# Odd batches tiled from token 64 in a sliding-window attention and spectral-mixing kernel

## The chip, the cores and the metric

The kernel runs on one core of one Trainium2 chip. The metric is the device time of one execution in microseconds. The engines are called as in the profile: PE (matmul), PEld (its weight loads, which overlap PE), DVE, ACT, POOL, and SP, which here only issues DMAs. A profile's times count from the start of its span.

## The reference

There are 8 batches, 8 heads, 576 tokens and a head width of 64. Each token attends to itself and the 127 before it, with a bias that falls off linearly with distance. The result x (8 x 576 x 512) is then mixed along the sequence in 64 Fourier modes:

```python
scores = scale * q @ k.T
mask = (rel >= 0) & (rel < 128)               # rel = query position - key position
scores = where(mask, scores - slope[h] * |rel|, -1e9)
x = softmax(scores) @ v                       # heads side by side: 8 x 576 x 512
X = rfft(x, axis=1)                           # of which 64 modes are kept
Y[:, m] = X[:, m] @ (w_r[m] + 1j * w_i[m])    # 64 complex matrices of 512 x 512
u = x + irfft(Y)
out = u + relu(u @ w_ch)
```

The weights w_r and w_i are 64 x 512 x 512 in float32 each, most of the 164 MB that are read.

## The kernel before

**Tiles of tokens.** 576 tokens are four tiles of 128 and one of 64. `g.x_sb` holds the four whole tiles of each batch, `g.x4` the rest: the last 64 tokens of an even batch in its partitions 0 to 63, those of the next, odd batch in 64 to 127. `g.seq` lists the 36 tiles in the order in which the tail works on them, with batch and first token of each half. `g.F` is the Fourier matrix with tokens on the partitions, one block of 128 for each tile; `g.FT` is its transpose for the way back, from which the tail takes 64 columns for each half of a tile.

**Attention.** A unit is two heads of one batch; there are 32, and batches go in pairs. For each pair d there are two slots (n = 2d and 2d + 1), in which `_slot` writes the work out by hand in this order on PE: scores of the first head (L436, after a filler matmul L417 that keeps PE going), transposes of the next pair's q and k (L377), transposes of v (L406), scores of the second head, more transposes, one batch's part of the spectrum (`_spectrum1`, L526), and `_av` (L467) for the pair before, the even batch in the even slot and the odd batch in the odd one. ACT does the exponential of the scores (L442) and copies most transposes out of PSUM (L387), DVE multiplies by the mask (L450) and divides by the sums (L483 to L489), POOL casts the loaded q, k and v to bf16 (L367). Scores have one PSUM buffer, and each engine works in the order written.

**`_av`.** A tile of 128 queries needs two tiles of keys: its own and the one before. So there are two matmuls for each tile and head but the first, each of 128 columns of attention (the stationary operand) and 65 columns of v with a column of ones. In the odd slot the shared tile follows: 64 columns for each batch, to partitions 0 to 63 and 64 to 127. That makes 14 matmuls in an even slot and 22 in an odd one.

**Weights.** They come through `g.wring`, a ring of three buffers of 18 KB per partition, filled by `_send` from SP's queue, in order with the loads of q, k and v (L356). Mode matrices for the first 128 channels are used during attention (`_modes`, L672, L620); the other three quarters follow in `_pair` (L703, L629) after it, while PE also transposes x (L726) and multiplies it with w_ch (L748).

**Tail.** After the last weights, `_finish` goes through the 36 tiles. Place i of the list decides how its result is added ("a": ACT and DVE; "q": ACT, DVE and POOL). `store` issues its stores on SP (L840, 256 KB; for a shared tile two of 128 KB, L842). The constants are set up once in `_consts` and `_consts2`.

Of the kernel before, what the change touches and what calls it, by code (L numbers as in the profile page):

```python
# [10 lines left out]
BF16 = mybir.dt.bfloat16  # L11
# [5 lines left out]
P = 128  # L17
# [16 lines left out]
def kernel(  # L34
# [10 lines left out]
    nc = tc.nc  # L45
    B, H, S, D = q.shape
    NM, DM, _ = moe_w_r.shape
# [3 lines left out]
    g = Ctx()  # L51
# [26 lines left out]

    g.FT = persist.tile([P, 4, S], BF16)
    g.F = persist.tile([P, ST, P], BF16)  # L80
    g.ident_b = persist.tile([P, P], BF16)
    g.ident2 = persist.tile([P, 64], BF16)
    g.wch = persist.tile([P, 4, DM], BF16)
# [5 lines left out]
    g.spectra = []  # L89
    g.seq = []  # L90
    for b in range(B):
        g.seq += [(g.x_sb[:, b, st], ((b, st * P), (b, st * P + 64))) for st in range(4)]
        if b % 2:
            g.seq.append((g.x4[:, b // 2], ((b - 1, 4 * P), (b, 4 * P))))
    g.way = ["q" if 2 <= i < len(g.seq) - 5 and i % 5 in (0, 2, 3) else "a" for i in range(len(g.seq))]

    with tc.manual_schedule(engines={ET.SP, ET.PE, ET.Activation, ET.DVE, ET.Pool}):
# [122 lines left out]
def _consts(g, tp):  # L220
    nc = g.nc
    NM, S, ST = g.NM, g.S, g.ST
    pi = tp.tile([P, 1], I32)
    nc.gpsimd.iota(pi, [[0, 1]], base=0, channel_multiplier=1)
    mi = tp.tile([P, 2, NM], I32)
    nc.gpsimd.iota(mi, [[0, 2], [1, NM]], base=0, channel_multiplier=0)
    make_identity(nc, g.ident_b)
    FAR = float(2**15)
    rel = tp.tile([P, 512], FP32)
    g.rel = rel  # L230
    both = rel.rearrange("p (a b) -> p a b", a=2)
    nc.gpsimd.iota(both, [[0, 2], [1, 256]], base=0, channel_multiplier=-1,
                   allow_small_or_imprecise_dtypes=True)
    for sign, base in ((1, 0), (-1, P - 1)):
        nc.gpsimd.affine_select(
            out=both, in_=both, compare_op=ALU.is_ge, fill=FAR, base=base,
            pattern=[[0, 2], [sign, 256]], channel_multiplier=-sign)
    tail = rel[:, 448:512]
    nc.gpsimd.iota(tail, [[1, 64]], base=64, channel_multiplier=-1,
                   allow_small_or_imprecise_dtypes=True)  # L240
    for base, step, mul in ((64, 1, -1), (-64, 0, 1)):
        nc.gpsimd.affine_select(
            out=tail, in_=tail, compare_op=ALU.is_ge, fill=FAR, base=base,
            pattern=[[step, 64]], channel_multiplier=mul)
    g.heads = list(range(1, g.H))

    pcol = tp.tile([P, 1], FP32)
    nc.vector.tensor_copy(pcol, pi)
    mrow = tp.tile([P, 2, NM], FP32)
    nc.vector.tensor_copy(mrow, mi)  # L250
    scol = tp.tile([P, ST], FP32)
    for st in range(ST):
        nc.vector.tensor_scalar_add(scol[:, st : st + 1], pcol, float(st * P))
    nc.vector.tensor_scalar_add(scol[64:128, 4:5], pcol[64:128], float(4 * P - 64))
    phrow = tp.tile([P, 2, NM], FP32)
    nc.vector.memset(phrow[:, 0, :], S / 4.0)
    nc.vector.memset(phrow[:, 1, :], S / 2.0)
    MAGIC = float(2**23)
    ang = tp.tile([P, ST * P], FP32)
    for st in range(ST):  # L260
        nc.vector.scalar_tensor_tensor(
            out=ang[:, st * P : (st + 1) * P],
            in0=mrow.rearrange("p a b -> p (a b)"),
            scalar=scol[:, st : st + 1], op0=ALU.mult,
            in1=phrow.rearrange("p a b -> p (a b)"), op1=ALU.add,
        )
    kf = tp.tile([P, ST * P], FP32)
    nc.vector.tensor_scalar_mul(kf, ang, 1.0 / S)
    nc.vector.tensor_scalar(kf, kf, MAGIC, -MAGIC, op0=ALU.add, op1=ALU.add)
    nc.vector.scalar_tensor_tensor(  # L270
        out=ang, in0=kf, scalar=-float(S), op0=ALU.mult, in1=ang, op1=ALU.add)
    nc.scalar.activation(
        g.F.rearrange("p a b -> p (a b)"), ang, AF.Sin, scale=2.0 * math.pi / S)
    g.one = pcol


def _consts2(g):
    nc = g.nc
    nc.gpsimd.tensor_tensor(
        out=g.ident2, in0=g.ident_b[:, 0:64], in1=g.ident_b[:, 64:128], op=ALU.add)  # L280
    nc.gpsimd.memset(g.pick, 0.0)
    one = g.ident_b.rearrange("p (q t) -> p q t", t=2)
    for h in range(2):
        for t in range(2):
            nc.gpsimd.tensor_copy(
                g.pick[:, h, t].rearrange("p (q t) -> p q t", t=2)[:, :, t], one[:, :, h])
    for vn in g.vns:
        nc.gpsimd.memset(vn[:, :, :, g.D : g.D + 1], 1.0)

# [163 lines left out]
def _av(g, d, e, av):  # L453


    nc = g.nc
    u = g.two[d]
    _, s, b = g.units[2 * d + e]
    D = g.D
    vn = g.vns[d % 2]  # L460

    def part(t, f, h, o, **kw):
        m = P if t < 4 else 64
        terms = [(t - 1, 256 * ((t - 1) % 2) + P)] if t else []
        terms.append((t, 256 * (t % 2) if t < 4 else 448))
        for i, (kt, c0) in enumerate(terms):
            nc.tensor.matmul(  # L467
                av[o, h, t * (D + 1) : (t + 1) * (D + 1)],
                lhsT=u.att[min(kt // 2, 1), h][:, f, c0 : c0 + m],
                rhs=vn[:, g.ST * h + kt, f, 0 : D + 1],  # L470
                start=(i == 0), stop=(i == len(terms) - 1), **kw)

    for h in range(2):
        for t in range(4):
            part(t, e, h, slice(0, P))
    n = 4 + e
    if e:
        for h in range(2):
            for f in range(2):
                part(4, f, h, slice(64 * f, 64 * f + 64), tile_position=(0, 64 * f))  # L480
    avv = av[:, :, 0 : n * (D + 1)].rearrange("p h (t c) -> p h t c", t=n)
    rec = g.work.tile([P, 2, n], FP32, tag=f"rec{e}", name="rec")
    nc.vector.reciprocal(rec, avv[:, :, :, D])  # L483
    xo = g.x_sb[:, b, :, s * P : (s + 1) * P].rearrange("p t (h d) -> p h t d", h=2)
    nc.vector.tensor_tensor(  # L485
        out=xo, in0=avv[:, :, 0:4, 0:D],
        in1=rec[:, :, 0:4].unsqueeze(-1).broadcast_to([P, 2, 4, D]), op=ALU.mult)
    if e:
        nc.vector.tensor_tensor(  # L489
            out=g.x4[:, b // 2, s * P : (s + 1) * P].rearrange("p (h d) -> p h d", h=2),  # L490
            in0=avv[:, :, 4, 0:D],
            in1=rec[:, :, 4].unsqueeze(-1).broadcast_to([P, 2, D]), op=ALU.mult)
# [10 lines left out]
def _spectrum1(g, j, b, a):  # L503

    nc = g.nc
    grp = GROUPS[j]
    ST = g.ST
    A = len(grp)
    po = 64 * (b % 2)
    ps = slice(po, po + 64)  # L510
    X = g.X[j]
    nb = 4 // A
    own = b == g.B - 1
    if own and a == 0:
        sc = g.ps2.tile([P, 2, 512], FP32, tag="sc", name="xtl")
        g.xt2 = sc[:, 0, 0 : A * 2 * g.NM].rearrange("p (k a i m) -> p k a i m", k=1, a=A, i=2)
    elif b % nb == 0 and a == 0:
        g.xt = g.ps2.tile([P, nb, A, 2, g.NM], FP32, tag="xt", name="xt")
    xt = g.xt2 if own else g.xt
    k = 0 if own else b % nb  # L520
    dc = slice(grp[0] * P + a, grp[0] * P + A * P, A)
    for st in range(ST):
        l = g.x_sb[:, b, st, dc] if st < 4 else g.x4[ps, b // 2, dc]
        f = g.F[:, st] if st < 4 else g.F[ps, st]
        kw = {} if st < 4 else dict(tile_position=(po, 0))
        nc.tensor.matmul(  # L526
            xt[:, k, a].rearrange("p i m -> p (i m)"), lhsT=l, rhs=f,
            start=(st == 0), stop=(st == ST - 1), **kw)
    if a < A - 1 or not own and b < g.B - 2 and k < nb - 1:
        return  # L530
    b0 = b - k
    if j:
        nc.vector.tensor_copy(X[:, :, :, b], xt[:, 0])
        return
    xi = xt[:, 0 : k + 1, 0].rearrange("p b i m -> p i b m")
    nc.vector.tensor_copy(X[:, 0, 1:3, b0 : b + 1], xi)
    nc.vector.tensor_scalar_mul(X[:, 0, 0, b0 : b + 1], xi[:, 1], -1.0)
# [283 lines left out]
def _finish(g):  # L821
# [5 lines left out]
    with ExitStack() as fctx:  # L827
        pool = fctx.enter_context(tc.tile_pool(name="fin", bufs=4))
        lps = fctx.enter_context(
            tc.tile_pool(name="lps", bufs=1, space=bass.MemoryType.PSUM, side="right"))  # L830
        first = [min(i for i, t in enumerate(g.seq) if t[1][0][0] == b and t[1][1][0] == b)
                 for b in range(g.B)]
        _z_late(g, 0, lps)
        _z_take(g, 0)
        o, r, y = {}, {}, {}

        def store(i):
            for h, (b, s) in enumerate(g.seq[i][1]):
                if h == 0 and g.seq[i][1][1] == (b, s + 64):
                    nc.sync.dma_start(out=g.out[b, s : s + P, :], in_=o[i])  # L840
                    break
                nc.sync.dma_start(out=g.out[b, s : s + 64, :], in_=o[i][64 * h : 64 * h + 64])  # L842

        for i in range(N + 3):
            if i < N:
# [62 lines left out]
```

## Time and profile before

| what | value |
|---|---|
| median of three runs | 444.44 us (443.52 to 445.49) |
| profiled execution | 445.46 us, its span 443.7 us |
| busy of the span | PE 72%, PEld 46%, DVE 50%, ACT 48%, POOL 23% |
| DMA | 173.73 MB, mean 392 GB/s |
| attention | to about 161 us (last L467) |
| weights of the other channels | to about 403 us |
| tail | from there to the end |
| matmuls on L467 | 576 |
| stores | 32 of 256 KB, 8 of 128 KB |

The shares of the span are means over three stages with different limits, so each stage has to be read by itself: in the windows view for its engines, and in the chain of waits for what ended last.

### The profile page before, as it was taken

To read this page: it belongs to the slowest core of one execution; us is meant where nothing else is said; L and a number is where in the kernel's file an instruction comes from. 1 tells how busy PE (TensorE), PEld (TensorE's weight loads), DVE (VectorE), ACT (ScalarE), POOL (GpSimd) and SP (SyncE) were. 2 spreads that over 40 slices of the span, in tenths; PEclk is the share of its full clock that TensorE was granted. 3 is DMA by queue.
4 is the path that set the end of the run, shared out by engine and by line. 5 is a ranking of instruction groups with operands and counts; after the bars stand their busy time and mean duration, and the time that the engine had idled before them with its cause. 6 is when DMAs were issued, how large, how long until landed. Compare 5 with 4: busy or idle time off the path is not lost.

```text
span 443.7 us, 10963 instructions
## 1 busy us (share of the span) xinstructions
PE 319.0 (72%) x4647; PEld 205.0 (46%) x4675; DVE 221.7 (50%) x404; ACT 214.8 (48%) x332; POOL 103.1 (23%) x156
## 2 busy tenths in 40 slices
PE   2778889899979878557564565554675587688994
PEld 1445566667757654334332333332333355344552
DVE  6466867778748723343332333323333345413784
ACT  4799968999969603222232212222122133302883
POOL 8844535555534102000000000000000000000882
PEclk9999978999969965687766858768658589966998
DMA  8999989999999999999999999999999999991787
GB/s 285 394 392 403 404 319 390 406 407 405 406 407 382 405 420 425 410 426 430 430 427 428 430 429 422 427 427 418 434 427 427 428 419 429 425 421 71 256 313 263
DMA packets 46145, 173.73 MB, mean 392 GB/s; under 512 B 3984, under 2 KB 3984, under 8 KB 38032
## 3 DMA queue, kind: packets, MB, share of 16 engines
q1 hardware_dynamic: 46096, 173.03, 96.9%
q8 instruction: 36, 0.59, 0.5%
q14 instruction: 13, 0.11, 0.1%
HBM read 163.58 MB, written 9.44 MB: 390 GB/s over the span
## 4 chain that ended last, share of the span: by engine, by line
DMA 56%; PE 21%; ACT 12%; DVE 6%; issue 3%; SPq 0%; POOL 0%; ACTq 0%; POOLq 0%
DMA wring<-in_moe_w_i_dram 33%; DMA wring<-in_moe_w_r_dram 23%; ACT att L442 5%; PE acc L703 4%; ACT T L387 4%; PE mm L735 3%; DVE att L450 2%; PE sc L436 2%; PE tqk L377 2%; PE y L735 2%; PE av L467 2%; PE acc L672 2%; PE av L406 1%; DVE x_sb L485 1%; ACT ys L865 1%
## 5 line engine op out<-in xcount | busy, mean ns | idle before, releaser
L752 ACT CAST hl<-xw 64x512 bf16<-64x512 f32 x72 | 41.7, 579 | 139.5 <-PE xw L748 101.2
L703 PE MATMUL acc<-Xz,wring 128*128 128x32 bf16 x1536 | 51.4, 183 | 72.1 <-DMA wring<-in_moe_w_i_dram 37.5
L703 PEld LDWEIGHTS <-wring 128*128 128x128 bf16 x1536 | 45.6, 101 | 103.9 <-DMA wring<-in_moe_w_i_dram 54.9
L753 DVE TENSOR_TENSOR hl<-xw,hl 64x512 bf16<-64x512 f32 x72 | 49.6, 688 | 79.2 <-ACT hl L752 79.0
L874 POOL TENSOR_TENSOR o<-r,ys 128x512 f32<-128x512 f32 x18 | 22.5, 1274 | 242.6 <-ACT ys L865 241.5
L450 DVE TENSOR_TENSOR att<-att,mask 128x1024 bf16<-128x1024 bf16 x64 | 55.2, 863 | 37.4 <-ACT att L442 36.8
L442 ACT ACTIVATE att<-sc 128x1024 bf16<-128x1024 f32 x64 | 67.0, 1047 | 10.0 <-PE sc L436 8.8
L387 ACT COPY T<-tqk 128x640 bf16<-128x640 bf16 x92 | 65.9, 773 | 1.7 <-PE tqk L377 1.7
L748 PE MATMUL xw<-wch,xT 128*128 128x512 bf16 x119 | 48.1, 522 | 4.7 <-issue 2.9
L377 PE MATMUL tqk<-ident_b,b 128*128 128x128 bf16 x432 | 39.5, 233 | 10.9 <-POOL b L367 6.4
L377 PEld LDWEIGHTS <-b 128*128 128x128 bf16 x432 | 27.3, 103 | 22.5 <-issue 11.0
L728 DVE COPY xT<-tp 128x512 bf16<-128x512 bf16 x36 | 15.1, 420 | 34.3 <-PE tp L726 34.2
L367 POOL CAST b<-v 128x576 bf16<-128x576 f32 x32 | 27.0, 869 | 16.4 <-issue 9.0
L436 PE MATMUL sc<-T,T 64*128 64x256 bf16 (+2 forms) x320 | 26.7, 264 | 2.3 <-ACT att L442 1.8
L367 POOL CAST b<-q 128x576 bf16<-128x576 f32 x32 | 21.4, 697 | 28.6 <-issue 28.6
L748 PEld LDWEIGHTS <-xT 128*128 128x128 bf16 x144 | 17.8, 129 | 21.3 <-issue 17.2
L367 POOL CAST b<-k 128x576 bf16<-128x576 f32 x32 | 22.0, 713 | 16.9 <-issue 8.7
L467 PE MATMUL av<-vn,att 128*128 128x65 bf16 (+1 forms) x576 | 24.5, 201 | 0.7 <-DVE x L489 0.4
L672 PE MATMUL acc<-X,wring 128*128 128x16 bf16 x488 | 18.9, 193 | 5.6 <-DMA wring<-in_moe_w_i_dram 5.2
L485 DVE TENSOR_TENSOR x_sb<-av,rec 128x512 bf16<-128x512 f32 x32 | 22.1, 691 | 1.1
L467 PEld LDWEIGHTS <-att 128*128 128x128 bf16 (+1 forms) x576 | 20.6, 104 | 3.7 <-DVE x L489 0.5
L406 PE MATMUL av<-ident_b,T 128*128 128x128 bf16 x160 | 15.1, 227 | 8.7 <-DVE x_sb L485 5.2
(106 smaller groups left out, 430.4 us busy)
## 6 DMA issues: line engine op xcount, KB each, us to landing
wring<-in_moe_w_r_dram SPq DMA_DIRECT2D x32, 1536.0 KB, 10.1
wring<-in_moe_w_i_dram SPq DMA_DIRECT2D x31, 1536.0 KB, 10.1
wring<-in_moe_w_i_dram SPq DMA_DIRECT2D x22, 768.0 KB, 8.9
wring<-in_moe_w_r_dram SPq DMA_DIRECT2D x20, 768.0 KB, 7.8
q<-in_q_dram SPq DMA_DIRECT2D x32, 288.0 KB, 6.4
k<-in_k_dram SPq DMA_DIRECT2D x32, 288.0 KB, 6.3
v<-in_v_dram SPq DMA_DIRECT2D x32, 288.0 KB, 6.3
out_dram<-o SPq DMA_DIRECT2D x32, 256.0 KB, 2.8
```

What stands on the lines that cost most here:

```text
L367: g.nc.gpsimd.tensor_copy(u.b[w][:, :, e], u.raw[w][e])
L377: g.nc.tensor.transpose(u.tp[:, r - r0], u.b[w][:, r].rearrange("p u d -> p (u d)"), g.ident_b)
L387: copy(u.T[w].rearrange("c h (p r) -> c (h p) r", r=g.R)[:, :, r0:r1], u.tp[:, 0 : r1 - r0].rearrange("c r p -> c p r"))
L436: nc.tensor.matmul(sc[:, e, c0 : c0 + nq], lhsT=kT[es, h, _start(kt) : _start(kt) + P], rhs=qT[es, h, kt * P : kt * P + nq], start=True, s ...
L442: nc.scalar.activation(a, sc, AF.Exp, scale=1.0 / math.sqrt(g.D))
L450: nc.vector.tensor_tensor(out=a, in0=a, in1=m, op=ALU.mult)
L467: nc.tensor.matmul(av[o, h, t * (D + 1) : (t + 1) * (D + 1)], lhsT=u.att[min(kt // 2, 1), h][:, f, c0 : c0 + m], rhs=vn[:, g.ST * h + kt, ...
L672: nc.tensor.matmul(acc[:, et, :, m - c0, :], lhsT=g.W[0, m, k][:, 0].bitcast(BF16)[:, 1::2][:, et * P : (et + 1) * P], rhs=X[:, 0, 1 - k : ...
L703: nc.tensor.matmul(acc[:, et, :, m - c0 : m - c0 + 2, :], lhsT=w[:, a].bitcast(BF16)[:, 1::2][:, et * P : (et + 1) * P], rhs=X[:, a, 1 - k ...
L748: nc.tensor.matmul(xw, lhsT=xT[:, dt], rhs=g.wch[:, dt], start=(dt == 0 and g.way[n] != "q"), stop=(dt == 3))
L752: nc.scalar.copy(g.hl[hi, n, h], xw[hi])
L753: nc.vector.tensor_tensor(out=g.hl[lo, n, h], in0=xw[hi], in1=g.hl[hi, n, h], op=ALU.subtract)
```

## The change

The tiles of odd batches begin at tokens 64, 192, 320 and 448. What an odd batch has over is then its first 64 tokens. Batches lie one behind the other in the output, so the last 64 rows of an even batch and the first 64 of the next are 128 neighbouring rows, and the shared tile is stored by one DMA. The shared tile moves ahead of the odd batch's tiles in `g.seq`.

For this the odd batch needs its own Fourier blocks (`g.F2`, two copies on POOL at the start). In `_av` a tile of an odd batch now meets three tiles of keys, which stay where they were: all 128 queries with the tile of the same number, the first 64 queries with the tile before, and the last 64 with the tile after. An odd slot has 30 matmuls in place of 22.

```diff
+    g.F2 = persist.tile([P, 4, P], BF16)
...
     for b in range(B):
-        g.seq += [(g.x_sb[:, b, st], ((b, st * P), (b, st * P + 64))) for st in range(4)]
         if b % 2:
-            g.seq.append((g.x4[:, b // 2], ((b - 1, 4 * P), (b, 4 * P))))
+            g.seq.append((g.x4[:, b // 2], ((b - 1, 4 * P), (b, 0))))
+        s0 = 64 * (b % 2)
+        g.seq += [(g.x_sb[:, b, st], ((b, s0 + st * P), (b, s0 + st * P + 64))) for st in range(4)]
...
-    nc.vector.tensor_scalar_add(scol[64:128, 4:5], pcol[64:128], float(4 * P - 64))
+    nc.vector.tensor_scalar_add(scol[64:128, 4:5], pcol[64:128], -64.0)
...
+    nc.gpsimd.tensor_copy(g.F2[0:64], g.F[64:128, 0:4])
+    nc.gpsimd.tensor_copy(g.F2[64:128], g.F[0:64, 1:5])
...
-    def part(t, f, h, o, **kw):
-        m = P if t < 4 else 64
-        terms = [(t - 1, 256 * ((t - 1) % 2) + P)] if t else []
-        terms.append((t, 256 * (t % 2) if t < 4 else 448))
-        for i, (kt, c0) in enumerate(terms):
+    def part(t, f, h, terms):
+        for kt, c0, o0, m, flags in terms:
+            kw = {} if m == P else dict(tile_position=(0, o0))
             nc.tensor.matmul(
-                av[o, h, t * (D + 1) : (t + 1) * (D + 1)],
+                av[o0 : o0 + m, h, t * (D + 1) : (t + 1) * (D + 1)],
                 lhsT=u.att[min(kt // 2, 1), h][:, f, c0 : c0 + m],
                 rhs=vn[:, g.ST * h + kt, f, 0 : D + 1],
-                start=(i == 0), stop=(i == len(terms) - 1), **kw)
-
+                start="a" in flags, stop="z" in flags, **kw)
+
+    col = [256 * (kt % 2) if kt < 4 else 448 for kt in range(g.ST)]
     for h in range(2):
         for t in range(4):
-            part(t, e, h, slice(0, P))
+            if e == 0:
+                terms = [(t - 1, col[t - 1] + P, 0, P, "a")] if t else []
+                terms.append((t, col[t], 0, P, "z" if t else "az"))
+            elif t == 0:
+                terms = [(0, 64, 0, 64, "az"), (0, P, 64, 64, "a"), (1, col[1], 64, 64, "z")]
+            else:
+                terms = [(t, col[t] + 64, 0, P, "a"), (t - 1, col[t - 1] + 192, 0, 64, "z"),
+                         (t + 1, col[t + 1], 64, 64, "z")]
+            part(t, e, h, terms)
...
         for h in range(2):
-            for f in range(2):
-                part(4, f, h, slice(64 * f, 64 * f + 64), tile_position=(0, 64 * f))
+            part(4, 0, h, [(3, col[3] + P, 0, 64, "a"), (4, col[4], 0, 64, "z")])
+            part(4, 1, h, [(0, 0, 64, 64, "az")])
...
-        f = g.F[:, st] if st < 4 else g.F[ps, st]
+        f = (g.F2 if b % 2 else g.F)[:, st] if st < 4 else g.F[ps, st]
...
         def store(i):
-            for h, (b, s) in enumerate(g.seq[i][1]):
-                if h == 0 and g.seq[i][1][1] == (b, s + 64):
-                    nc.sync.dma_start(out=g.out[b, s : s + P, :], in_=o[i])
-                    break
-                nc.sync.dma_start(out=g.out[b, s : s + 64, :], in_=o[i][64 * h : 64 * h + 64])
+            (b, s), _ = g.seq[i][1]
+            nc.sync.dma_start(out=rows[b * g.S + s : b * g.S + s + P], in_=o[i])
```

Here `rows` is the output as 8 x 576 rows in one list. The first tile of each batch in the list, by which the tail takes over late results, is now the first that holds any of the batch; its places in the list stay the same.

More of the change, by code (lines that the diff above doesn't have):

```diff
@@ L830, in _finish @@
             tc.tile_pool(name="lps", bufs=1, space=bass.MemoryType.PSUM, side="right"))
-        first = [min(i for i, t in enumerate(g.seq) if t[1][0][0] == b and t[1][1][0] == b)
+        first = [min(i for i, t in enumerate(g.seq) if b in (t[1][0][0], t[1][1][0]))
                  for b in range(g.B)]
@@ L835, in _finish @@
         o, r, y = {}, {}, {}
+        rows = g.out.rearrange("b s d -> (b s) d")
         def store(i):
-            for h, (b, s) in enumerate(g.seq[i][1]):
-                if h == 0 and g.seq[i][1][1] == (b, s + 64):
-                    nc.sync.dma_start(out=g.out[b, s : s + P, :], in_=o[i])
-                    break
-                nc.sync.dma_start(out=g.out[b, s : s + 64, :], in_=o[i][64 * h : 64 * h + 64])
+            (b, s), _ = g.seq[i][1]
+            nc.sync.dma_start(out=rows[b * g.S + s : b * g.S + s + P], in_=o[i])
         for i in range(N + 3):
```

## The prediction

> **What bounds the kernel now.** I read the windows first, then the chain of waits, then the timelines at the lines that the diff touches. Windows (columns: PE, PEld, DVE, ACT, POOL busy us, granted clock, DMA share, GB/s) for attention, a hole in it, and two stretches of the tail:
>
> ```profile
> 24.00:60.00 36.00, 29.28 (x440) 20.32 (x439) 26.93 (x49) 34.75 (x48) 18.44 (x26) 1.00 1.05 400
> 62.00:64.00 2.00, 2.00 (x37) 1.27 (x34) 0.05 (x1) 0.49 (x2) 0.00 (x0) 0.51 0.24 87
> 64.50:122.00 57.50, 53.59 (x926) 39.66 (x924) 43.97 (x78) 54.94 (x76) 30.57 (x42) 0.96 1.04 401
> 122.60:124.60 2.00, 0.00 (x0) 0.00 (x0) 1.27 (x2) 0.68 (x2) 0.73 (x2) 0.72 1.04 399
> 432.50:434.50 2.00, 2.00 (x22) 1.28 (x20) 1.75 (x3) 1.66 (x3) 2.00 (x3) 1.00 0.47 116
> 434.50:441.00 6.50, 3.12 (x30) 1.74 (x26) 3.50 (x6) 2.48 (x5) 1.19 (x1) 0.99 1.03 380
> ```
>
> DMA is full nearly throughout, but attention also has ACT at 35 of 36 us and PE at 93% after 64. At 62 to 64 the loads run dry: compute came late to free the weight ring. At 122.6 PE waits for weights instead. So two bounds run level, and whichever falls behind sets the end. The chain in order of time says when DMA takes over:
>
> ```profile
> 98.28 9.65 DMA wring<-in_moe_w_i_dram
> 108.00 8.11 DMA wring<-in_moe_w_i_dram
> 116.17 8.40 DMA wring<-in_moe_w_i_dram
> 124.62 0.89 PE acc L672 x23
> ```
>
> Each of these loads is 768 KB, 1.94 us at 405 GB/s, yet takes 8.1 to 9.7 us to land: some 6.2 us of other loads are queued ahead. Until that queue is used up, late compute costs DMA nothing. From 151 to 403 the chain is weight loads, so time lost to an idle DMA before 151 is not made up.
>
> Now the attention-times-values matmuls of an odd slot (weight loads, PE, ACT; three answers of the timeline):
>
> ```profile
> 54.83 0.48 PEld L467 LDWEIGHTS <-att 128*128 128x128 bf16 x14
> ...
> 55.36 0.21 PEld L467 LDWEIGHTS <-att 128*64 128x64 bf16 x8
> 55.61 0.09 PEld L417 LDWEIGHTS <-ident_b 128*32 128x32 bf16 x1
> ...
> 54.84 0.84 PE L467 MATMUL av<-vn,att 128*128 128x65 bf16 x22
> 55.61 0.39 PE L417 MATMUL sc<-F,ident_b 128*32 128x512 bf16 x1
> 55.94 0.39 PE L436 MATMUL sc<-T,T 64*128 64x256 bf16 x4
> ...
> 54.87 1.38 ACT L387 COPY T<-tqk 128x640 bf16<-128x640 bf16 x2
> 56.37 1.02 ACT L442 ACTIVATE att<-sc 128x1024 bf16<-128x1024 f32 x1
> ```
>
> Fourteen 128-column loads start over 0.48 - 0.095 us (one load's length), so 13 steps of 0.0295 us. The last starts at 55.215; the first 64-column one only at 55.36: a step of 0.15 between loads, and of 0.123 between the matmuls themselves (55.242 to 55.365 in the trace). The same step is 0.122 to 0.124 in all 13 cases at full clock and 0.173 in the three at half clock, with no wait on it. Inside the 64-column group neighbours on different halves start 0.007 us apart, the next pair 0.024 later. So changing the tile shape costs 0.094 us over staying in it, and swapping halves costs none.
>
> **The change, attention.** For an even batch nothing changes. For an odd batch, 22 matmuls become 30, and the order is 3 of 64 columns, then 128, 64, 64 three times, all that for each head, then six of 64. That is 12 changes of shape inside the run instead of one; the changes into and out of it stay at one each. Before: 13 x 0.0295 + 0.10 (the eight of 64) + 0.12 = 0.60 us of starts. After: 12 x 0.122 + 17 steps among 64-column matmuls at about 0.015 = 1.46 + 0.25 = 1.71. So +1.1 us for each of 16 runs at full clock, about +1.5 at half clock (0.173 for a change). The other direction, 64 to 128, appears inside attention only as L467 to L672: 0.128, taken as the same.
>
> The Trainium skill, TensorEngine Tiling (Array Packing), Key Properties, says that changing the tiling mode, and not just the tile, drains TensorE; the 0.123 against 0.007 and 0.029 us here bears that out.
>
> Who waits: queued behind the run on PE are L417 and the next scores; ACT waits for these. Above, scores end at 56.33, ACT starts at 56.37, having been free since 56.25. After all four odd runs before 60 us (28.9, 37.8, 46.3, 54.8), ACT starts the exponential 0.04 to 0.09 us after the last score matmul. With ACT at 96% nothing gives it back: 4 x 1.1 = **+4.4 us** on the ring's release at 62.87, and DMA, dry from 62, waits as much longer. (Bounds: 3.6, if 0.2 of each were free, to 4.6.)
>
> From 64 to 122 there are seven more runs, one at half clock: 1.5 + 6 x 1.1 = 8.1 us late, of which the queue of loads swallows 6.2: **+1.9 us**. The last five (128, 137, 145, 153, 160: 5.5 us) I put at nothing. Their cover is the 2.0 us at 122.6 where PE waits now and need not then, the half clock that follows that wait (the windows give 0.67 for 120 to 130; about 2.4 us), and PE idle 3.2 us of 151 to 160. Bounds for these twelve runs: 0 (all covered) to 13.6 (none).
>
> **Start-up.** POOL gets two copies of 64x512 bf16 (F2), after the pick copies and before the casts of the second pair:
>
> ```profile
> 10.44 0.78 POOL L285 COPY pick<-ident_b 128x64 bf16<-128x64 bf16 x4
> 11.14 0.27 POOL L288 MEMSET vn<- 128x20 bf16 x2
> 11.24 1.27 POOL L367 CAST b<-q 128x576 bf16<-128x576 f32 x2
> 12.46 1.78 POOL L367 CAST b<-k 128x576 bf16<-128x576 f32 x2
> 15.82 0.67 POOL L367 CAST b<-v 128x576 bf16<-128x576 f32 x1 [1.57 <-DMA v<-in_v_dram]
> ```
>
> Nearest rows: 0.2 (L285) to 0.9 us (L367) each, so 0.4 to 1.8. I take 1.2, nearer the casts in elements. F has been ready since 7.78, and POOL waits 1.57 us for v anyway. The q cast would end near 13.7, its transposes start at 13.89: **0**, up to 0.4 at the top price. The changed constant in scol, F2 in place of F as operand, and the new offsets into FT keep their shapes: 0.
>
> **Tail.** The four shared tiles move from places 8, 17, 26, 35 to 4, 13, 22, 31, with each place's way of computing unchanged; eight 64-row stores become four of 128. On SP the two half stores take 0.5 to 1.2 us of issue each, a whole one 0.39 at the median. At 432.43 and 432.95 the halves of tile 26 hold up tile 25, ready since 431.64, and then tile 27, while DMA moves 116 GB/s; from 434.5 to 441 it drains at 380 to 404. Those two stores would issue 0.8 to 0.97 us sooner, and the final one is one issue instead of two (439.12 and 439.65). The drain then starts sooner by **-0.8 us** (bounds 0, if only the 404 GB/s counts, and -1.0). The bytes are the same.
>
> **Sum.** The profiled execution took 445.46 us (span 443.7, 1.76 around it), 1.02 over the median of three. 445.46 + 4.4 + 1.9 + 0 - 0.8 = 450.96; less 1.02: **450.0 us**.
>
> **Rivals.** *No cover.* Queue and idle PE swallow nothing, because each late release also delays the loads behind it on SP: 444.44 + 4.4 + 8.1 + 5.5 - 0.8 = 461.6. For it: ACT and PE stand at 93 to 97%; against: 2.56 MB are outstanding at most ring loads after 77.
>
> *Hidden.* PE's extra time costs nothing: 443.6. For it: DMA is at 1.05 in attention. Against: the dry hole at 62 and the 0.04 us between score and ACT. The same page's section Theoretical Speedup gives up to twice the rate to 64-wide tiles; were that all, 12 pairs and 6 whole matmuls would equal the old 14 and 4 pairs, and this rival would hold; the 0.123 us rows speak against it.
>
> *The store queue (faster).* SP sets the tail at all four shared tiles. Their pairs take 1.19 + 1.77 + 1.11 + 1.51 = 5.58 us against 4 x 0.39 = 1.56: -4.0, so 440.4 with attention hidden. It gives a gain over 0.5% only if attention costs under 1.8 us. For: SP is hardly idle after 426.5; against: SP's waits in the tail are 14.6 us for DVE's tiles.
>
> *Not as it says.* The changed program's order of instructions has 36 whole stores and 704 matmuls on that line, so this is out; that the stores bring nothing would be 450.8.
>
> **Chances.** Forecast (447 to 453): 0.60. Little or no cover (453 to 462): 0.20; worse still 0.04. Hidden: 0.10. Store queue: 0.06. The range 446 to 458 takes in the forecast, the near part of "hidden" and two thirds of "little cover". Half a per cent, about what this kernel's three runs (443.52 to 445.49) can tell from nothing, is 2.2 us: faster 0.06, same 0.10, slower 0.84.
>
> **What would show it.** Right: the L467 run of an odd slot lasts 1.9 to 2.0 us instead of 0.84; ACT's idle before L442 grows by about 1 us in every odd slot; the dry hole after 62 grows to 6 or 7 us; the last weights land near 409 in the span; the tail from there is 0.8 us shorter. Wrong: the run stays under 1.2 us, or the hole stays at 2 us, or the last weights land within 1 us of 402.8.

## The result and the profile after

The changed kernel takes 460.92 us (456.07 to 462.49, six runs), the one before 445.23 beside it: 1.0341 of its time, 95% interval 1.0309 to 1.0373. That is slower, as forecast, but by 15.7 us and not 5.6, and outside the range. The profiled execution took 460.83 us, its span 459.1. In the experiments below three executions (457.5 and 470.82 us of one kernel, 463.08 of another) fell in a slower state and are left out of the medians and ratios.

The attention-times-values run of an odd slot is now this (timeline of the kernel after; weight loads, then PE, then ACT; a merged row bears the shape of its first instruction, so the x30 rows hold both shapes):

```profile
58.32 2.14 PEld L469 LDWEIGHTS <-att 128*64 128x64 bf16 x30
60.50 0.09 PEld L421 LDWEIGHTS <-ident_b 128*32 128x32 bf16 x1
...
58.41 2.16 PE L469 MATMUL av<-vn,att 128*64 128x65 bf16 x30
60.50 0.39 PE L421 MATMUL sc<-F,ident_b 128*32 128x512 bf16 x1
60.82 0.39 PE L440 MATMUL sc<-T,T 64*128 64x256 bf16 x4
...
58.36 1.37 ACT L391 COPY T<-tqk 128x640 bf16<-128x640 bf16 x2
61.26 1.02 ACT L446 ACTIVATE att<-sc 128x1024 bf16<-128x1024 f32 x1 [1.53 <-PE sc L440]
```

2.16 us instead of 0.84, and ACT waits 1.53 us for the scores behind it, where it waited 0.12. In the windows the loads now run short over most of attention (columns as in the prediction):

```profile
66.00:70.00 4.00, 3.85 (x65) 2.90 (x66) 0.96 (x4) 1.62 (x3) 0.52 (x1) 0.58 0.32 82
69.00:98.00 29.00, 26.59 (x347) 18.90 (x344) 16.12 (x29) 21.20 (x28) 12.50 (x16) 0.74 0.94 347
69.00:126.00 57.00, 53.27 (x728) 38.52 (x725) 33.54 (x59) 43.11 (x59) 25.83 (x34) 0.81 0.92 331
```

331 GB/s over 57 us, against the 405 that a full queue moves, is as much as 10.4 us without any load. The clock column, 0.81 (0.74 up to 98), is lower too. SP's timeline gives the times at which the ring's first half was free for the next load, one for each pair of slots:

```profile
67.73 0.38 SPq L631 DMA_DIRECT2D wring<-in_moe_w_r_dram  x1
...
76.82 0.38 SPq L631 DMA_DIRECT2D wring<-in_moe_w_r_dram  x1
...
87.31 0.38 SPq L631 DMA_DIRECT2D wring<-in_moe_w_r_dram  x1
...
97.47 0.38 SPq L631 DMA_DIRECT2D wring<-in_moe_w_r_dram  x1
```

They are 9.1 to 10.5 us apart. Before the change the same loads left at 62.87, 70.09, 77.83, 85.83 and 93.94, about 8 us apart. The last weights land at 420.73 (402.77 before): 18.0 us later, 4.9 of it there at the first release. The tail gives back 2.6: from those weights to the end 38.33 us (40.89).

### The profile page after: what moved, and what is told of

Same layout as the page of the kernel before. It is cut to its first block, busy times and chain, and to the rows that moved or that the text cites. A ratio compares the mean times of both kernels' runs of the same rounds, so it can differ in the third digit from the quotient of the medians.

```text
span 459.1 us, 11217 instructions
## 1 busy us (share of the span) xinstructions
PE 343.3 (75%) x4775; PEld 222.5 (48%) x4803; DVE 222.3 (48%) x404; ACT 215.3 (47%) x332; POOL 105.9 (23%) x158
## 4 chain that ended last, share of the span: by engine, by line
DMA 42%; PE 36%; ACT 11%; DVE 5%; issue 3%; POOL 3%; SPq 0%; POOLq 0%; ACTq 0%
DMA wring<-in_moe_w_i_dram 22%; DMA wring<-in_moe_w_r_dram 20%; PE av L469 9%; ACT att L446 5%; PE acc L714 4%; PE tqk L381 3%; PE sc L440 3%; ACT T L391 3%; PE acc L683 3%; DVE att L454 2%; PE mm L746 2%; PE xt L537 2%; PE y L746 2%; PE sc L421 2%; PE av L410 2%
## 5 line engine op out<-in xcount | busy, mean ns | idle before, releaser
L759 PE MATMUL xw<-wch,xT 128*128 128x512 bf16 x119 | 50.0, 540 | 4.9 <-issue 3.1
L381 PE MATMUL tqk<-ident_b,b 128*128 128x128 bf16 x432 | 41.2, 240 | 11.6 <-POOL b L371 8.3
L469 PE MATMUL av<-vn,att 128*128 128x65 bf16 (+1 forms) x704 | 47.1, 211 | 1.4 <-DVE vn L414 1.0
L469 PEld LDWEIGHTS <-att 128*128 128x128 bf16 (+1 forms) x704 | 35.6, 108 | 12.2 <-issue 1.0
L381 PEld LDWEIGHTS <-b 128*128 128x128 bf16 x432 | 28.4, 106 | 24.1 <-issue 11.2
L371 POOL CAST b<-q 128x576 bf16<-128x576 f32 x32 | 23.3, 757 | 47.0 <-issue 46.8
L440 PEld LDWEIGHTS <-T 64*128 64x128 bf16 x320 | 11.6, 96 | 16.6 <-issue 12.2
```

The costliest lines, as they stand in the source:

```text
L371: g.nc.gpsimd.tensor_copy(u.b[w][:, :, e], u.raw[w][e])
L381: g.nc.tensor.transpose(u.tp[:, r - r0], u.b[w][:, r].rearrange("p u d -> p (u d)"), g.ident_b)
L440: nc.tensor.matmul(sc[:, e, c0 : c0 + nq], lhsT=kT[es, h, _start(kt) : _start(kt) + P], rhs=qT[es, h, kt * P : kt * P + nq], start=True, s ...
L469: nc.tensor.matmul(av[o0 : o0 + m, h, t * (D + 1) : (t + 1) * (D + 1)], lhsT=u.att[min(kt // 2, 1), h][:, f, c0 : c0 + m], rhs=vn[:, g.ST ...
L759: nc.tensor.matmul(xw, lhsT=xT[:, dt], rhs=g.wch[:, dt], start=(dt == 0 and g.way[n] != "q"), stop=(dt == 3))
```

## The experiments

Of the numbers below, ratios are against the kernel before on the same chip; microseconds worked out from them use its 444.8.

**The order of the matmuls.** The 30 matmuls stay, but the six of 128 columns of both heads come first and the 24 others after them, neighbours on different halves. Only the first matmul of a head carries a start flag ("a"); the later ones carry none:

```diff
+    if e and d not in MIXED:                  # MIXED = ()
+        for h in range(2):
+            for t in range(1, 4):
+                part(t, 1, h, [(t, col[t] + 64, 0, P, "a" if t == 1 else "")])
+        for h in range(2):
+            for t in range(1, 4):
+                part(t, 1, h, [(t - 1, col[t - 1] + 192, 0, 64, ""), (t + 1, col[t + 1], 64, 64, "")])
+            part(0, 1, h, [(0, 64, 0, 64, ""), (0, P, 64, 64, "")])
+            part(4, 0, h, [(3, col[3] + P, 0, 64, "")])
+            part(0, 1, h, [(1, col[1], 64, 64, "")])
+            part(4, 0, h, [(4, col[4], 0, 64, "z")])
+            part(4, 1, h, [(0, 0, 64, 64, "z")])
```

> The changed kernel with the odd slot's 30 matmuls in another order: the six of 128 columns of both heads first, then the 24 of 64 columns, neighbours on different halves; one change of shape inside the run instead of 12, the same 30 matmuls, stores, F2 and list. If the changes of shape make the loss: the run of an odd slot lasts about 0.8 to 0.9 us (2.16 now), and the time is 444 to 446. If the eight added matmuls themselves make it (or the new Fourier blocks, or the order of the list), it stays at 456 to 462.

Measured: 443.52 us, ratio 0.9971 (0.9949 to 0.9992). Its weight loads of one run:

```profile
55.27 0.74 PEld L470 LDWEIGHTS <-att 128*128 128x128 bf16 x30
56.05 0.09 PEld L422 LDWEIGHTS <-ident_b 128*32 128x32 bf16 x1
```

30 loads in 0.74 us, the PE run 0.85. So the eight added matmuls, the new Fourier blocks and the list cost nothing that can be measured; the order of shapes cost all 17 us (16.5 by the ratios). This version is 0.3% faster than the kernel before, and the interval only just leaves out no difference.

**Shapes alone, in the kernel before.** Its eight 64-column matmuls are set between those of 128, none is added (abridged):

```diff
+            for kt, c0 in terms:              # t = 0..3, 128 columns each
+                if kt == 3 and t == 3:
+                    half(1, h, 4, 448)        # 64 columns of the shared tile
+                nc.tensor.matmul(... start=(t == 0), stop=(kt == 3))
+            if t < 3:
+                half(t % 2, h, 3 + t // 2, 384 if t < 2 else 448)
```

> The kernel before with the eight 64-column matmuls of an odd slot set one by one between those of 128: 16 changes of shape inside the run instead of one, no matmul added, tiles and stores as before. If a change costs what the trace shows (0.12 to 0.15 a step): the run lasts 2.4 us (0.84), 1.6 us more, and with three quarters of it reaching the end, as in the changed kernel (15.7 of 16 x 1.32), the time is about 464; if all of it does, 470. If the added matmuls make the loss, it stays near 445.

Measured: 471.76 us, ratio 1.0641 (1.0579 to 1.0702), 28 us slower without one more matmul. The timeline shows each change (PE, part of a run):

```profile
51.90 0.19 PE L490 MATMUL av<-vn,att 128*128 128x65 bf16 x1
52.02 0.22 PE L474 MATMUL av<-vn,att 128*64 128x65 bf16 x1
52.17 0.24 PE L490 MATMUL av<-vn,att 128*128 128x65 bf16 x2
52.33 0.22 PE L474 MATMUL av<-vn,att 128*64 128x65 bf16 x1
```

From 51.90 to 52.02 and on to 52.17: 0.12 to 64 columns and 0.15 back. Then two of 128 take 0.16 to the next change. At full clock a run lasts 2.62 us, 1.78 more than 0.84; 16 of them are 28.5 us, as much as the whole loss (28.5 by the ratio, 27.0 by the medians). The start flags are not the cause: this kernel also has only one for each head, as the grouped order has, and its run takes 2.62 us where that one's takes 0.85. Nor is it that two matmuls in a row add to the same place, since the 64-column ones here write columns of their own.

**Where in attention.** Five kernels keep the twelve changes in some odd slots and the grouped order in the others:

```diff
-MIXED = ()
+MIXED = range(4)          # first four; others: range(11, 16), range(4, 11), (4, 5, 6), (8, 9, 10)
```

> As the grouped order, but the first four odd slots (before the first modes' weights are used) keep the changed kernel's order with 12 changes. Lateness before the ring is freed for the first time is not covered by anything: 4 x 1.3 = 5.2 us above the grouped order. If the queue of loads covers it: no difference.

Measured: 448.70 us, ratio 1.0118 (1.0076 to 1.016): 5.2 us over the grouped order by the medians, 6.5 by the ratios. Nothing covers there.

> As the grouped order, but the last five odd slots keep the 12 changes. By the prediction's step (PE's waits there cover them): within 1 us of the grouped order. If nothing covers: 5 x 1.3 = 6.5 us above it.

Measured: 447.17 us, ratio 1.0065 (1.0022 to 1.0107): 3.6 us over it by medians, 4.2 by ratios. The prediction's zero for these five was wrong; something between half and two thirds of their 5 x 1.32 = 6.6 us reaches the end. How much is not sharp: the seven runs go from 444.0 to 450.33, and the profiled one, 445.66, lost only about 1.1 us there (390 GB/s on average from 130 to 160, against 405 in the grouped order), with its queue thinner but never dry.

> As the grouped order, but the seven odd slots from about 66 to 117 us keep the 12 changes, 7 x 1.3 = 9.1 us of PE time, one of them at half clock. If the queue of loads (2.56 MB, 6.2 us) swallows what it holds: 3 us above the grouped order. If the losses of the parts simply add (17.4 in all, less 5.2 and 3.6): 8.6 us above.

Measured: 450.12 us, ratio 1.0108 (1.0076 to 1.0141): 6.1 us by the ratios, between the two forecasts, and twice the 2.9 us that a standing queue of 6.2 would leave. By ratios the three parts come to 6.5 + 6.1 + 4.2 = 16.8 us, the whole is (1.0341 - 0.9971) x 444.8 = 16.5: they add, as far as parts known to 1.5 to 2 us each can show it.

> As the grouped order, but only the three odd slots right after the hole (66 to 84 us) keep the 12 changes: 3.9 us of PE time, added while the queue of loads is still being built up (0.3 MB at 63, 1.8 at 70, 2.56 from 78). If a queue that is not yet there covers nothing: 3 to 4 us above the grouped order; if cover is the same everywhere: as much as the three late ones.

> As the grouped order, but only the three odd slots from 100 to 117 us keep the 12 changes: 3.9 us of PE time, with 2.56 MB (6.2 us) outstanding at each ring load there. If the queue covers once it stands: within 1 us of the grouped order. If nothing is ever covered: 3.9 us above it.

Measured: 449.54 us (ratio 1.0074, 1.0037 to 1.0111) for the three early ones and 443.24 us (0.9961, 0.9939 to 0.9983) for the three late ones. By the ratios the same added PE time costs 4.6 us over the grouped order in one place and nothing in the other. The windows of the early ones, then of the late ones:

```profile
69.00:98.00 29.00, 26.69 (x353) 18.84 (x353) 16.53 (x30) 20.44 (x27) 11.10 (x15) 0.77 0.93 338
```

```profile
69.00:98.00 29.00, 25.71 (x484) 18.97 (x482) 22.60 (x40) 28.45 (x40) 15.43 (x22) 1.00 1.04 402
99.00:122.00 23.00, 22.67 (x372) 16.84 (x369) 16.01 (x28) 18.87 (x27) 9.88 (x14) 1.00 1.05 405
```

The late ones leave DMA at 405 GB/s even in their own stretch; the early ones bring it to 338. Outstanding at the ring loads, from the trace, with every load counted whole until it has landed: 2.56 MB or more throughout in the late case, 1.77, 0.89 and 0.59 MB at 72, 83 and 93 us in the early one. Counted by the packets that had not yet moved, it is 1.6 to 2.5 MB from 99 to 122 us in the late case, and 0.68, 0.08 and 0.02 MB in the early one, so there the queue is empty. So the queue covers, but only where it stands. It is built between 63 and 78, right after the hole, by a pair of slots that frees the ring (after 7.2 us) faster than its 3.34 MB are loaded (8.25 us at 405 GB/s).

**The clock.** Filler matmuls go ahead of the first modes, where PE sits idle (abridged, with two operands renamed):

```diff
+        if m == 0:
+            for _ in range(5):
+                nc.tensor.matmul(acc_as_32x512, lhsT=g.ident_b[:, 0:32], rhs=F_first_512, start=True, stop=True)
```

> The changed kernel with five filler matmuls of 512 columns ahead of the first modes, where PE sits idle for about 1 us before its clock is granted at half from 66.6 to 80.3. If that half clock is part of the loss: it stays at full clock there, and the time is 2 to 5 us under the changed kernel's 460.9. If the fillers only delay: 0 to 1 us above it.

> The seven middle odd slots with 12 changes, as in the kernel that was 6 us above the grouped order, and the five filler matmuls ahead of the first modes. Two things can have kept the queue of loads from covering: the half clock that follows the idle PE after the hole, and that a pair of slots with 12 changes takes longer (9.2 us in the warm kernel) than its loads (3.34 MB, 8.25 us at 405 GB/s), so that no queue builds up at all. If the clock is all of it: within 2 us of the grouped order's 443.5. If a pair is too slow even at full clock: 7 x about 1 us, less what the end of attention gives back, so 446 to 449.

Measured: in the changed kernel 453.14 us (ratio 1.0214, 1.0144 to 1.0285), by the ratios 5.6 us less; in the kernel with the middle seven 450.74 us (1.0121, 1.0078 to 1.0164), no change from its 1.0108 without fillers, and above the 446 to 449 forecast. In the first one's profile the clock stays full from 35 to 167 us, and the ring is freed at 68.27, 75.50, 84.57, 93.80 and 103.21: from the second on every 9.1 to 9.4 us at full clock, still more than 8.25. In the second one's profile the clock is at half at 69 to 76 and 79 to 82 in spite of the fillers, so this run does not tell the clock from the pace. What can be said is that a pair with twelve changes is too slow for its loads at full clock too, and that half clock made the changed kernel worse. The queue that comes about at full clock is used up again: by the packets, 1.09, 0.98, 0.61 and 0.32 MB are outstanding at the four releases from 75.50 to 103.21.

**The tail and the start.** Grouped order, with the shared tiles in two stores again, or with the F2 copies moved to slot 3; the best parts with the fillers; and the kernel before with only its list reordered (abridged):

```diff
+                for h in range(2):            # split stores, at a shared tile
+                    nc.sync.dma_start(out=rows[r0 + 64 * h : r0 + 64 * h + 64], in_=o[i][64 * h : 64 * h + 64])
...
+    if n == 3:                                # late copies, no longer in _consts2
+        g.nc.gpsimd.tensor_copy(g.F2[0:64], g.F[64:128, 0:4])
+        g.nc.gpsimd.tensor_copy(g.F2[64:128], g.F[0:64, 1:5])
...
+        if b % 2:                             # the list alone, in the kernel before
+            g.seq.append((g.x4[:, b // 2], ((b - 1, 4 * P), (b, 4 * P))))
         g.seq += [(g.x_sb[:, b, st], ((b, st * P), (b, st * P + 64))) for st in range(4)]
-        if b % 2:
-            g.seq.append((g.x4[:, b // 2], ((b - 1, 4 * P), (b, 4 * P))))
```

> The grouped order with the four shared tiles stored in two DMAs of 64 rows each (at places 4, 13, 22 and 31). The prediction's tail step gave 0.8 us to the single stores: 0.5 to 0.8 us above the grouped order, if it is the issue on SP; less than that, if most of the gain is that the last place of the list is now a whole tile, which this kernel keeps.

> The grouped order with the two F2 copies moved on POOL from the constants to slot 3, ahead of the first odd batch's spectrum. In the traces the first run of attention times values is 0.4 us later than before the change. If the copies at the start make that: 0.4 us under the grouped order (443.5), so about 443; if it is POOL's 3 us of slack there that hides them: the same.

> The grouped order with the fillers and the late F2 copies, the best parts together. If the half clock after the hole costs the grouped order nothing, since loads are queued there soon: 442 to 443.5, as without the fillers. If it still costs: 1 to 2 us less.

> The kernel before, with tiles, matmuls and split stores as they were; only the list puts each shared tile ahead of the odd batch's tiles, as in the changed kernel. If the end of the tail gains because the last place is a whole tile with one store and not two: the stretch from the last o to the end of the span falls from 4.9 to 3.9 us, and the time by about 1 us, to 443.8. If it is the single store of shared tiles in general: no change.

Measured: split stores 443.38 us, ratio 0.9969 (0.995 to 0.9988), as without the split. Late copies 442.79, ratio 0.9956 (0.9931 to 0.9981), not to be told from the grouped order. With the fillers and the late copies 443.83, ratio 0.9976 (0.9956 to 0.9996): the clock there stays full from the hole to 125 us, where the grouped order has 6.8 us of half clock from 64.4, and nothing is gained, so the half clock costs nothing where the queue comes to stand. List alone 444.57, ratio 0.9986 (0.9965 to 1.0008), unclear by its time. From the end of the last o to the end of the span it has 4.04 us, before 4.90. The last DVE and SP lines of the list-only kernel:

```profile
438.70 0.69 DVE L871 TENSOR_TENSOR o<-y,r 128x512 f32<-128x512 f32 x1 [0.17 <-ACT r L862]
...
436.09 1.11 SPq L842 DMA_DIRECT2D out_dram<-o  x2
437.30 2.78 SPq L840 DMA_DIRECT2D out_dram<-o  x5
```

The last split store is now five stores from the end. After the last o the changed kernel has 3.82 us, the grouped one 3.88, the grouped one with split stores 3.93. So in the profiles the end of the tail gains about 1 us because the last place is a whole tile, whether shared tiles go out in one store or two; in the time of the list-only kernel the gain is not clear of the noise.

## Why the prediction was wrong, and where it was right

Term by term, with the measured part by the ratios behind each: first four runs +4.4 (6.5), seven middle runs +1.9 (6.1), last five 0 (4.2), all else -0.8 (-1.3, the grouped order). That makes 15.5 of the measured 15.7 us.

**Right: what costs.** The step "changing the tile shape costs 0.094 us" was the cause, in kind and nearly in size. A change measured 0.133 towards 64 columns and mostly 0.150 back (0.122 and 0.128 had been taken), so a run grew by 1.32 us, not 1.1. Added matmuls are free, as the rows of 0.007 us between halves had said; the rival "hidden" failed as its counter-evidence said. By its size alone, 1.32 in place of 1.1, this term added some 3.5 us of PE time over the 16 runs.

**Right: the first four runs.** +4.4 was forecast for the first release; it came 4.86 us later in the profile (67.73 for 62.87), and the experiment on these four gives 5.2 to 6.5 us.

**Wrong: "of which the queue of loads swallows 6.2: +1.9".** This is the step that failed: the seven middle runs cost 6.1 us. Two things were wrong in it. First, the 6.2 us were read off at 98 us and then spent from 64 us on. At 64 there is no queue, since the hole has just emptied it. It comes about because a pair of slots is for a while faster than its loads; with twelve changes a pair takes, from the second one after the hole on, 9.1 us or more against 8.25, and what has formed is used up. The three late runs show that a queue which stands covers 3.9 us.

Second, 6.2 us is too much even for a standing queue. It was taken as the time to landing less the 1.94 us of the load's own transfer, but a load that finds nothing outstanding does not land after 1.94 us: the one issued at 67.73 in the changed kernel took 4.0 us, the one at 62.87 in the kernel before 4.5. That leaves about 4 of the 8.1 us for the queue. The packets say the same: from 86 to 106 us in the kernel before, 1.6 to 1.7 MB were still to be moved at the first load of each ring buffer, about 4 us at 405 GB/s. The 2.56 MB of the prediction counts loads whole that had partly landed.

**Wrong: the last five at nothing.** With 2.4 MB or more outstanding, loads counted whole, at the ring loads of that stretch in the grouped kernel, they still cost about 4 us in the median. Three covers were named (PE's wait at 122.6, the half clock behind it, PE's idle time from 151 to 160); which of them fails was not taken apart and stays open.

**The rival "no cover"** gave 461.6, 0.7 from the measured time. It gave as its reason that late releases delay the loads behind them on SP. The runs don't show that reason: with a standing queue the same late releases cost nothing. Its 461.6 also took all twelve runs at full price with a step of 1.1, two errors that offset one another: 16 x 1.32 would be 21.1, of which 16.5 arrived. That it came so close is luck.

**The tail's -0.8** had about the right size at its end (-1.1 after the last o, in the profiles) from only one of the two reasons given; the single stores at the earlier places bring nothing. The rival of the store queue is out: with eight split stores the time is the same. The whole tail was 2.6 us shorter in the profile. The other 1.5 us go with the clock: in the first part of the tail it was at half before (0.67 over 400 to 410), for about half as long after. From the last weights to the last o the tail took 36.00 us with 6.8 us of half clock (before), 34.51 with 3.4 (after), and 33.44 in the two profiles that had none (split stores; the changed kernel with fillers).

**Start-up at 0.** The copies took 0.61 us each, and POOL's wait for v is gone:

```profile
11.01 0.61 POOL L289 COPY F<-F 64x512 bf16<-64x512 bf16 x1
11.66 0.61 POOL L290 COPY F<-F 64x512 bf16<-64x512 bf16 x1
12.32 0.27 POOL L292 MEMSET vn<- 128x20 bf16 x2
12.43 1.81 POOL L371 CAST b<-q 128x576 bf16<-128x576 f32 x2
14.19 1.27 POOL L371 CAST b<-k 128x576 bf16<-128x576 f32 x2
15.41 1.32 POOL L371 CAST b<-v 128x576 bf16<-128x576 f32 x2
```

The v cast starts at 15.41, even before the 15.82 of the kernel before. The first run of attention times values is 0.4 us later than before, but so it is with the copies moved away (25.14) and in the list-only kernel without copies (25.07): it is not theirs.

## What to carry to other kernels

Count changes of tile shape, not matmuls: here one change costs more than three matmuls of 65 columns, and sorting the matmuls by shape took 17 us off. Work that is late is covered by a queue only if the queue stands at that moment; look at what is outstanding when a buffer is freed, and ask whether the period of the ring, with the change in it, is still shorter than its loads. Once it is longer, a queue that stands is used up and one that doesn't stand never lasts, and from then on the difference is paid in every round. And the time from issue to landing is not all queue: compare it with a load that found the queue empty.

## What the runs showed of the hardware

The change back from 64 to 128 columns costs more than the change to 64 (0.150 against 0.133 at full clock, 0.19 against 0.164 at half). Two 64-column matmuls on different halves start 0.003 to 0.004 us apart in the changed kernel, so the second one costs next to nothing. A 768 KB load took 4.0 us from issue to landing with nothing outstanding, and 8.1 to 9.7 behind a standing queue. And a wait can come with a second cost: after the hole PE's clock was at half for 13.7 us (6.8 before), in the very stretch in which the queue should have formed. With fillers in PE's 1.0 us of idle there the clock stayed full in two kernels of three, so that the idle brings the half clock is likely but not shown.
